# Keys 64-127 meet only tokens 64-127: scores, P times V and k times v as 64x64 quarters, in two parts

## The chip, the core and the metric

The kernel runs on one NeuronCore of a Trainium2 chip. Its engines each work through a queue of their own and meet at semaphores: TensorE (PE, with its weight loads shown apart as PEld), VectorE (DVE), ScalarE (ACT), GpSimd (POOL) and SyncE (SP, which here only issues DMAs). The metric is the device time of one execution in microseconds (us). A profile is one execution in which every instruction's start and end were recorded; its span runs from the first instruction to the last.

## The reference

Two stages, all in float32. The first is an mLSTM cell over 4 batches x 8 heads x 768 tokens, head size 40:

```python
for t in range(S):
    m_new = maximum(f[t] + m, i[t]);  f_s = exp(f[t] + m - m_new);  i_s = exp(i[t] - m_new)
    C = f_s * C + i_s * outer(v[t], k[t]);  n = f_s * n + i_s * k[t]
    y[t] = sigmoid(o[t]) * (C @ q[t]) / maximum(abs(n @ q[t]), 1.0)
```

Its output, as 3072 tokens x 320, goes through a feed-forward layer (FFN): `h = maximum(x @ w_in, 0)`, result `(h * h) @ w_out`, with 2048 hidden columns.

## The kernel before

**Chunks.** The recurrence over tokens is worked in 24 chunks `s` of 128 tokens, 6 to a batch. Within a chunk, key token p acts on token t with the weight exp(A[t] + b[p]) where t is not before p, and with nothing where it is. `A` is a running sum of the gates per head, `b` a per-key term. For each chunk the kernel forms the scores k.q (all keys against all tokens), multiplies them by the weights (this product is called P), multiplies P by v, adds what the state C of earlier chunks gives (q scaled by exp(A), times C), and makes the next C from k times the weighted v. A column of ones beside v carries n along with C. Each chunk's scores are a full 128x128 square per head, half of which the weights set to zero: in the 64x64 quarter of keys 64-127 and tokens 0-63 all of it.

**Chunks 6 to 23**, where the change lies, run in the loop over `parts` (line 1091), four parts to a chunk (`at` = 0 to 3). `s = 6 + n // 4`. Each part also holds a quarter of an FFN stage for an earlier group of two chunks, written as seven products for eight (Strassen's way). In even chunks from 8 on it is the second layer (`ffn2_fast`, products at line 766); in odd ones the first layer (`ffn1_open`, `ffn1_close`, blocks at line 842, and `ffn1_rows`, line 891, which does the last 64 input columns as 64x64 quarters of the array).

**Order.** The program's order on every engine is the order in which it is written; no scheduler moves it. For an even chunk s, part 0 holds `scores(s)` and `weighted(s)`; part 1 begins with `scores(s + 1)` and `attend_turned(s)`; part 2 holds `weighted(s + 1)`. For an odd chunk part 1 begins with the FFN's `ffn1_rows`, then `attend_turned(s)`.

**What the lines do.**
- `load` (line 311), `load_part` (line 943), `load_A` (line 348): DMAs of k, v and of A's rows, the last copied to all 128 partitions (8 heads x 128 tokens each). All are issued on SP. `pair_up` (line 301) copies k and q into a scratch tensor by DMAs of POOL's queue from chunk 10 on; `load_squares` and `turn_kq` make the transposed `kT`, `qT` from it, heads 0-3 in partitions 0-63, heads 4-7 in 64-127.
- `decays` (line 382, ACT): exp(A) in that layout, before the mask; `mask` (line 375, POOL): A is set to -1e30 where the token is before the key; `weigh` (line 390, ACT): exp(A + b), one instruction of 128x128 per head; `values` (line 409, POOL): the weighted v, `vw`.
- `scores` (line 436): from chunk 7 on, 16 matmuls (4 heads of a half x 2 halves of keys x 2 halves of heads), each 40 rows x 64 columns of weights, streaming 128 tokens. Its rows are one partition half and its output another, so four are in the array at a time.
- `weighted` (line 458, DVE): P, two instructions of 128x512.
- `attend_turned` (line 526): 8 matmuls of C (line 543), in quarters; 8 of P times V (line 552), 128 rows of keys x 64 columns, two at a time; 8 of k times v (line 562), 128 rows x 40 columns, streaming 41, two at a time. Then DVE transposes (line 569) and the new C (line 575).
- `store_num`, `load_num`, `normalise_turned`, `store_rows`, `load_rows`, `turn_squares`: the result goes through DRAM to be turned, is normalised and gated, and becomes the FFN's input.
- Before the loop come chunks 0 to 5 with another form of attention, the FFN's first two groups, and the rounding of the weights; `turn_rows(5)` (copy at line 654) and `ffn1_begin` (copies at line 855) stand where the one passes into the other.

PSUM: `ps_at` has three banks (tag "at") for scores and attention's outputs, `ps_h` five in the loop for the FFN and, in part 1, for odd chunks' scores.

Of the kernel before, what the change touches and what calls it, by code (L numbers as in the profile page):

```python
# [17 lines left out]
P = 128  # L18
# [11 lines left out]
def kernel(  # L30
# [64 lines left out]
    A_d = nc.dram_tensor("a_rows", (BH, S), F32, kind="Internal").ap()  # L95

# [157 lines left out]
    eA_T = consts.tile([P, B, NB, H], F32)  # L254

# [42 lines left out]
    KQ_SQ, X_SQ = 7, 6  # L298
    HALVES = slice(0, DP), slice(DP, 2 * DP)

    def pair_up(s):
        b, c = divmod(s, NB)
        eng = nc.sync if s < 10 else nc.gpsimd
        for n, src in enumerate((k, q)):
            for i in range(2):
                eng.dma_start(
                    kq_d[s, i, n].rearrange("j (m r) d -> m j (r d)", r=8),
                    src[b, PR * i : PR * (i + 1), c * P : (c + 1) * P, :].rearrange("j (m r) d -> m j (r d)", r=8),
                )

    def load(s):
        b, c = divmod(s, NB)
        (dk, sk), nat_q, vv = load_parts(s)
        for dst, src in ((dk, sk), nat_q, vv) if s < KQ_SQ else ((dk, sk), vv):
            nc.sync.dma_start(dst, src[b, :, c * P : (c + 1) * P, :].rearrange("h p d -> p h d"))
# [32 lines left out]
    def load_A(s):  # L348
# [3 lines left out]
        d["A"] = [A]  # L352
        nc.sync.dma_start(
# [21 lines left out]
    def mask(s):  # L375

        A = st[s]["A"][0]
        nc.gpsimd.affine_select(  # L378
            A[:], A[:], compare_op=ALU.is_ge, fill=-1e30, base=0, pattern=[[0, H], [1, P]], channel_multiplier=-1,
        )  # L380

    def decays(s):

        if s % NB > 0:
            e = st[s]["eA"] = kq_b[2 + s % 2][:, 1].rearrange("p (j two) d -> p j (two d)", two=2)
            for i in range(2):
                rows = slice(DP * i, DP * (i + 1))
                nc.scalar.activation(e[rows], st[s]["A"][0][rows, PR * i : PR * (i + 1), :], AF.Exp)  # L388

    def weigh(s, masked=False):  # L390
# [8 lines left out]
        for i in range(len(A)):  # L399
# [9 lines left out]
    def values(s):  # L409
        b, c = divmod(s, NB)  # L410
        d = st[s]
        if c + 1 < NB:
            d["vw"] = prep.tile([P, H, D1], F32, name="vw")
            nc.gpsimd.tensor_tensor(  # L414
# [21 lines left out]
    def scores(s, o=(False, False)):  # L436
# [4 lines left out]
        if s >= KQ_SQ:  # L441
            for j in range(PR):
                for keys in HALVES:
                    for i in range(2):
                        rows = slice(DP * i, DP * i + D)
                        nc.tensor.matmul(  # L446
                            sc[i][keys, j, :], lhsT=d["kT"][rows, j, keys], rhs=d["qT"][rows, j, :], start=(j == 0),
                            stop=True, skip_group_check=True,
                        )
# [8 lines left out]
    def weighted(s):  # L458
        d = st[s]
        d["P"] = []  # L460
        for i in range(2):
            heads = slice(i, H, 2) if s < KQ_SQ else slice(PR * i, PR * (i + 1))
            t = d["W"][:, heads, :]
# [4 lines left out]
            nc.vector.tensor_tensor(t, d["sc"][i], d["W"][:, heads, :], op=ALU.mult)  # L468
# [57 lines left out]
    def attend_turned(s):  # L526

# [3 lines left out]
        halves = [slice(DP * i, DP * (i + 1)) for i in range(2)]  # L534
        live = [slice(DP * i, DP * i + D) for i in range(2)]
        numT = [ps_at.tile([P, W], F32, name="numT", tag="at")[:].rearrange("p (c t) -> p c t", t=P) for _ in range(2)]

        if c > 0:
            C = C_b[(s - 1) % 2]
            for e in range(2):  # L540
                for i, g in ((0, 0), (1, 1), (0, 1), (1, 0)):
                    j = 2 * e + g
                    nc.tensor.matmul(  # L543
                        numT[i][halves[g], e, :], lhsT=C[live[i], j * D1 : j * D1 + DP], rhs=d["eA"][live[i], j, :],
                        start=(e == 0), stop=False, skip_group_check=True,
                    )
        for i in range(2):
            for e in range(2):
                for g in range(2):
                    j = 2 * e + g  # L550
                    h = PR * i + j
                    nc.tensor.matmul(  # L552
                        numT[i][halves[g], e, :], lhsT=va_w[s % NKQ][:, h * D1 : h * D1 + DP],
# [675 lines left out]
```

## Time and profile before

| what | value |
|---|---|
| median of 6 runs | 503.38 us (501.31 to 504.5) |
| the profiled execution | 502.71 us, span 500.9 us |
| PE busy | 493.3 us (98%) |
| DVE / ACT / POOL busy | 354.4 (71%) / 249.2 (50%) / 151.1 us (30%) |
| DMA | 67.75 MB, mean 135 GB/s; 185600 of 235551 packets under 512 B |

A matmul of the code is two records of PE and two of PEld, since float32 is passed twice. Matmuls overlap in the array: a record's own length (0.27 us for a quarter) is longer than the step from one group to the next, so the starts are read, not the lengths. The "idle before" of a group counts only while its engine had nothing; an idle engine off the path costs nothing. Line numbers are those of the kernel before unless a text says otherwise.

### The profile page before, as it was taken

To read this page: it belongs to the slowest core of one execution; us is meant where nothing else is said; L and a number is where in the kernel's file an instruction comes from. 1 tells how busy PE (TensorE), PEld (TensorE's weight loads), DVE (VectorE), ACT (ScalarE), POOL (GpSimd) and SP (SyncE) were. 2 spreads that over 40 slices of the span, in tenths; PEclk is the share of its full clock that TensorE was granted. 3 is DMA by queue.
4 is the path that set the end of the run, shared out by engine and by line. 5 is a ranking of instruction groups with operands and counts; after the bars stand their busy time and mean duration, and the time that the engine had idled before them with its cause. 6 is when DMAs were issued, how large, how long until landed. Compare 5 with 4: busy or idle time off the path is not lost.

```text
span 500.9 us, 13846 instructions
## 1 busy us (share of the span) xinstructions
PE 493.3 (98%) x5640; PEld 458.0 (91%) x5641; DVE 354.4 (71%) x646; ACT 249.2 (50%) x492; POOL 151.1 (30%) x194
## 2 busy tenths in 40 slices
PE   9989999999999999999999999999999999999997
PEld 4877878897799999999999999999999999999997
DVE  8589969879967866767867856867857956735441
ACT  3867878854541660771661770561871560423400
POOL 3355733431525224215225224234224031020000
PEclk9998999999999999999999999999999999999999
DMA  9999898855778758767758757767745522200000
GB/s 190 216 227 214 241 217 156 223 97 98 158 158 167 152 118 173 158 140 161 157 114 178 156 112 170 165 127 170 160 96 141 114 67 65 61 23 14 1 27 27
DMA packets 235551, 67.75 MB, mean 135 GB/s; under 512 B 185600, under 2 KB 229120, under 8 KB 235488
## 3 DMA queue, kind: packets, MB, share of 16 engines
q1 hardware_dynamic: 233600, 62.09, 59.2%
q0 software_dynamic: 1792, 4.59, 3.1%
q8 instruction: 44, 0.72, 0.6%
q10 hardware_dynamic: 96, 0.20, 0.1%
q14 instruction: 19, 0.16, 0.1%
HBM read 54.56 MB, written 17.86 MB: 145 GB/s over the span
## 4 chain that ended last, share of the span: by engine, by line
PE 91%; DVE 5%; DMA 2%; ACT 1%; issue 1%; SPq 0%; DVEq 0%
PE h_ps L766 34%; PE h_ps L842 25%; PE h_ps L891 8%; PE numT L552 4%; PE h_ps L712 4%; PE h_ps L675 3%; PE hp L491 2%; PE h_ps L446 2%; PE tp L446 2%; PE numT L543 1%; PE tp L454 1%; DVE mag L225 1%; DMA va<-in_v_dram 1%; PE dC L562 1%; PE A_ps L369 1%; PE tp L431 1%
## 5 line engine op out<-in xcount | busy, mean ns | idle before, releaser
L378 POOL TENSOR_SCALAR_AFFINE_SELECT A_bc<-A_bc 128x1024 f32<-128x1024 f32 x22 | 27.1, 1234 | 108.5 <-ACT kq L388 87.0
L766 PE MATMUL h_ps<-T,S 128*128 128x160 f32 x352 | 51.4, 299 | 0.0
L872 ACT COPY r_sb<-h_ps 128x512 f32<-128x512 f32 x18 | 10.5, 586 | 81.8 <-PE h_ps L842 81.8
L766 PE MATMUL h_ps<-w_out,g 128*128 128x160 f32 x336 | 49.2, 303 | 0.0
L782 DVE TENSOR_TENSOR y_sb<-y_sb,h_ps 128x160 f32<-128x160 f32 x44 | 14.1, 320 | 49.6 <-PE h_ps L766 49.6
L766 PEld LDWEIGHTS h_ps<-T,S 128*128 128x128 f32 x352 | 49.0, 190 | 0.0
L766 PEld LDWEIGHTS h_ps<-w_out,g 128*128 128x128 f32 x336 | 46.1, 190 | 1.4 <-issue 1.2
L402 ACT ACTIVATE A_bc<-A_bc,b_T 128x128 f32<-128x128 f32 x144 | 44.0, 388 | 5.3 <-POOL A_bc L378 5.0
L842 PE MATMUL h_ps<-xT,w_in 128*128 128x128 f32 x320 | 42.8, 278 | 0.0
L842 PE MATMUL h_ps<-lent_t,w_in 128*128 128x128 f32 x320 | 42.2, 275 | 0.0
L842 PEld LDWEIGHTS h_ps<-xT,w_in 128*128 128x128 f32 x320 | 38.9, 192 | 1.1 <-issue 0.7
L891 PE MATMUL h_ps<-xT,w_in 64*64 64x128 f32 x960 | 39.4, 273 | 0.0
L842 PE MATMUL h_ps<-lent_t 128*128 128x128 f32 x320 | 39.0, 275 | 0.0
L842 PEld LDWEIGHTS h_ps<-lent_t,w_in 128*128 128x128 f32 x320 | 38.9, 192 | 0.0
L842 PEld LDWEIGHTS h_ps<-lent_t 128*128 128x128 f32 x320 | 37.3, 192 | 0.0
L891 PEld LDWEIGHTS h_ps<-xT,w_in 64*64 64x64 f32 x960 | 34.6, 133 | 2.4
L569 DVE STREAM_TRANSPOSE tn<-numT 128x256 f32<-128x256 f32 x36 | 16.0, 450 | 28.8 <-PE numT L552 28.8
L414 POOL TENSOR_TENSOR vw<-va,A_bc 128x328 f32<-128x328 f32 x15 | 13.7, 913 | 72.5 <-issue 38.1
L909 DVE TENSOR_TENSOR r_sb<-r_sb,h_ps 128x512 f32<-128x512 f32 x20 | 13.8, 688 | 23.7 <-PE h_ps L842 14.3
L675 PE MATMUL h_ps<-xT,w_in 128*128 128x256 f32 x128 | 29.8, 386 | 0.6 <-ACT xT L654 0.6
L766 PE MATMUL h_ps<-w_out,g_c 128*128 128x160 f32 x192 | 28.0, 302 | 0.0
L675 PEld LDWEIGHTS h_ps<-xT,w_in 128*128 128x128 f32 x128 | 24.1, 193 | 4.1 <-ACT xT L654 0.8
(190 smaller groups left out, 1115.5 us busy)
## 6 DMA issues: line engine op xcount, KB each, us to landing
A_bc<-a_rows SPq DMA_DIRECT2D x22, 512.0 KB, 5.0
num_rows<-tn SPq DMA_DIRECT2D x18, 256.0 KB, 2.2
kq<-num_rows SPq DMA_DIRECT2D x72, 64.0 KB, 1.9
raw<-in_moe_w_out_dram SPq DMA_DIRECT2D x7, 640.0 KB, 4.2
kqT<-kq_rows SPq DMA_DIRECT2D x34, 128.0 KB, 3.0
kq<-in_k_dram SPq DMA_DIRECT2D x24, 160.0 KB, 3.8
va<-in_v_dram SPq DMA_DIRECT2D x24, 160.0 KB, 5.1
og<-in_o_gate_dram SPq DMA_DIRECT2D x24, 160.0 KB, 4.8
```

What stands on the lines that cost most here:

```text
L378: nc.gpsimd.affine_select(A[:], A[:], compare_op=ALU.is_ge, fill=-1e30, base=0, pattern=[[0, H], [1, P]], channel_multiplier=-1,)
L402: nc.scalar.activation(d["W"][:, i * n + h, :], A[i][:, h, :], AF.Exp, bias=b_T[:, b, c, i * n + h : i * n + h + 1],)
L446: nc.tensor.matmul(sc[i][keys, j, :], lhsT=d["kT"][rows, j, keys], rhs=d["qT"][rows, j, :], start=(j == 0), stop=True, skip_group_check=True,)
L552: nc.tensor.matmul(numT[i][halves[g], e, :], lhsT=va_w[s % NKQ][:, h * D1 : h * D1 + DP], rhs=d["P"][h % 2][:, h // 2, :] if s < KQ_SQ els ...
L569: nc.vector.transpose(to[:, 2 * i : 2 * i + 2], numT[i][:, :2, :].rearrange("p c t -> p (c t)"))
L675: nc.tensor.matmul(hs[i][:, n, :], lhsT=w_in[:, a, fb * P : (fb + 1) * P], rhs=xT[:, :, a, :], start=(n == 0 and a == 0), stop=False,)
L712: nc.tensor.matmul(o_ps, lhsT=st["g2", g][:, fb, j * P : (j + 1) * P], rhs=w_out[:, fb, :], start=(fb == 0), stop=(fb == NF - 1),)
L766: nc.tensor.matmul(to, lhsT=lhsT[:, p], rhs=rhs[:, p, :], start=(start and p == 0), stop=(p == NPAIR - 1), skip_group_check=True,)
L782: add = lambda to, a, b: nc.vector.tensor_tensor(to, a, b, op=ALU.add)
L842: nc.tensor.matmul(to[:, n, :], lhsT=lhsT[:, 4 * q + n, :], rhs=rhs, start=(start and n == 0), stop=True, skip_group_check=True,)
L891: nc.tensor.matmul(to[cols, n, :], lhsT=w_in2[rows, 4 * q + n, cols], rhs=rhs, start=(start and n == 0), stop=True, skip_group_check=True,)
L909: tt(U2[:], U2[:], Y[:], op=ALU.add)
```

## The change

From chunk 8 on (`ROT = 8`), keys 64-127 are multiplied with tokens 64-127 only, and scores, P times V and k times v are all cut into 64x64 quarters of the array. To fill four quarters at once, the data are laid out anew:

- Heads are numbered anew within their halves (`pair_up` takes every second head).
- `load_k` swaps the two token halves of heads 4-7 (three DMAs for one); `load_v` puts v into slots by key half (four DMAs for one, on SP for chunks 8 to 10, on POOL's queue from 11 on; issued a part later than before in half of the chunks).
- A's rows stand in a second scratch tensor `a_slots`, which three DMAs of POOL's queue fill per batch (`spread_slots`), before the loop, and in chunks 8 and 12; `load_A` reads it in two DMAs of contiguous rows.
- `mask` is two instructions of 64 partitions; `weigh` is 4 instructions of 128 columns and 4 of 64, with biases from a table `b_R`, which four ACT copies of 64x96 make just before the loop; `decays` is four instructions of half the width; `weighted` works on 384 columns instead of 512; `normalise_turned` has two more DVE instructions.

On PE `attend_turned` becomes two parts. `attend_begin`: half of C's matmuls, P times V of the early keys' pairing (wide), half of k times v. `attend_end`: the other half of k times v, the late keys' P times V (64 columns), the other half of C. Both parts add into the same PSUM bytes from different row halves of the array. Between them stands other PE work: the scores of the odd chunk in even chunks, `ffn1_rows` in odd ones, nothing in chunk 7. A DVE instruction on one element, issued at the end of `attend_begin`, reads from the first part's output; the first instruction of the second part that overwrites that place waits for it. Chunks 6 and 7 take the two parts too, at full width.

The core of the diff:

```diff
@@ scores
         if s >= KQ_SQ:
-            for j in range(PR):
-                for keys in HALVES:
-                    for i in range(2):
-                        rows = slice(DP * i, DP * i + D)
-                        nc.tensor.matmul(sc[i][keys, j, :], lhsT=d["kT"][rows, j, keys], rhs=d["qT"][rows, j, :], ...)
+            for e in range(2):
+                for late_keys in range(2):
+                    for c in range(2):
+                        for i in range(2):
+                            rows = slice(DP * i, DP * i + D)
...
+                                j, keys = 2 * (c ^ late_keys) + e, HALVES[late_keys]
+                                to = d["sc"][i][HALVES[c], e, slice(0, DP) if late_keys else slice(DP, 3 * DP)]
+                                t0 = DP * late_keys
+                            nc.tensor.matmul(to, lhsT=d["kT"][rows, j, keys], rhs=d["qT"][rows, j, t0:], ...)
@@ attend_turned becomes attend_begin and attend_end
+    def attend_begin(s):
...
+        out = d["out"] = [ps_at.tile([P, W], F32, name="numT", tag="at") for _ in range(2)]
...
+        if c > 0:
+            values_of_C(s, (0, 1))
+        for i in range(2):
+            values_of_P(s, i, (0, 1), False)
+        if c + 1 < NB:
+            new_C(s, (0, 1), False)
+            end, spare = out[1][DP : DP + 1, 2 * P + D1 : 2 * P + D1 + 1], d["kq"][DP : DP + 1, 0, 2, DP - 1 :]
+        else:
+            end, spare = out[1][DP : DP + 1, P : P + 1], C_b[(s - 1) % 2][0:1, 4 * D1 : 4 * D1 + 1]
+        nc.vector.tensor_scalar(spare, end, scalar1=0.0, scalar2=None, op0=ALU.mult)
...
+    def values_of_P(s, i, rows, second):
+        d = st[s]
+        t0 = DP if second and s >= ROT else 0
+        for e in range(2):
+            for m in range(2):
+                at, keys = slot(s, m, e, i, second), HALVES[rows[m]]
...
+                nc.tensor.matmul(
+                    d["numT"][m][HALVES[e], i, t0:], lhsT=va_w[s % NKQ][keys, at * D1 : at * D1 + DP], rhs=rhs, ...)
+
+    def new_C(s, rows, second):
+        d = st[s]
+        for e in (1, 0) if second else (0, 1):
+            for i in range(2):
+                for m in range(2):
+                    keys = HALVES[rows[m]]
+                    nc.tensor.matmul(
+                        d["dC"][m][HALVES[i], e, :], lhsT=d["kq"][keys, 0, 4 * m + 2 * e + i, :],
+                        rhs=d["vw"][keys, slot(s, m, e, i, second), :], start=False, stop=True, ...)
+
+    def attend_end(s):
...
+        if c + 1 < NB:
+            new_C(s, (1, 0), True)
+        else:
+            values_of_C(s, (1, 0), (1, 0))
+        for i in (1, 0):
+            values_of_P(s, i, (1, 0), True)
+        if 0 < c < NB - 1:
+            values_of_C(s, (1, 0))
@@ load_k, load_v, spread_slots, load_A
+        nc.sync.dma_start(dst[:, :PR], src[:, :PR])
+        for n in range(2):
+            nc.sync.dma_start(dst[HALVES[n], PR:], src[HALVES[1 - n], PR:])
...
+        eng = nc.sync if s < 11 else nc.gpsimd
+        for n in range(2):
+            for late_keys in range(2):
+                m = n ^ late_keys
+                eng.dma_start(dst[HALVES[n], PR * (1 - late_keys) : PR * (2 - late_keys)],
+                              src[HALVES[late_keys], PR * m : PR * (m + 1)])
...
+        nc.gpsimd.dma_start(A_slots[b].rearrange("c m x own t -> (m x) c own t")[:, :, 1], rows)
+        for m in range(2):
+            nc.gpsimd.dma_start(to[1 - m][:, :, 0], rows[PR * m : PR * (m + 1)])
...
+            for m in range(2):
+                nc.sync.dma_start(A[HALVES[m]].rearrange("p h t -> p (h t)"),
+                    A_slots[b, c, m].rearrange("x own t -> (x own t)").unsqueeze(0).to_broadcast([DP, H * P]))
@@ weigh, weighted
+        for x in range(PR if s >= ROT else 0):
+            for own, to in enumerate((slice(DP, P), slice(P, 2 * P))):
+                nc.scalar.activation(A[0][:, x, to], A[0][:, x, to], AF.Exp, bias=b_R[:, b, c, own, x : x + 1])
...
-            nc.vector.tensor_tensor(t, d["sc"][i], d["W"][:, heads, :], op=ALU.mult)
+            nc.vector.tensor_tensor(t, d["sc"][i], d["W"][:, heads, :] if s < ROT else t, op=ALU.mult)
@@ before the loop
+    for m in range(2):
+        for own in range(2):
+            x = PR * (m ^ own ^ 1)
+            nc.scalar.copy(b_R[HALVES[m], :, :, own], b_T[HALVES[1 - own], :, :, x : x + PR])
+    spread_slots(1)
@@ the loop, part 1
         if at == 1:
+            do(attend_begin, s)
             if even:
                 do(lambda s: scores(s, ("h", "h")), s + 1)
             if fast:
                 ffn1_rows(g, 0, True)
-            do(attend_turned, s)
+            do(attend_end, s)
...
-                do(lambda s: load_part(s, 0), s + 4)
+                do(load_k, s + 4)
...
         if s > 6 and at == (3 if even else 2):
             do(pair_up, s + 3)
+            do(load_v, s + 4)
+        if n in (9, 25):
+            spread_slots(2 + n // 25)
```

## The prediction

> **What bounds the kernel now.** I read first the page: busy shares, slices, the chain that ended last.
>
> ```profile
> span 500.9 us, 13846 instructions
> PE 493.3 (98%) x5640; PEld 458.0 (91%) x5641; DVE 354.4 (71%) x646; ACT 249.2 (50%) x492; POOL 151.1 (30%) x194
> ...
> PEclk9998999999999999999999999999999999999999
> ...
> PE 91%; DVE 5%; DMA 2%; ACT 1%; issue 1%; SPq 0%; DVEq 0%
> ```
>
> TensorE is busy 98% of the span, holds 91% of the chain, and its granted clock stays at full speed. "Busy" is modelled, so I asked next for PE's waits: over the span five, 4.4 us together, all in lines of the opening part (484, 653, 675, the idle matmuls); from 100 us to the end, not one. From there the time is the sum of PE's steps: what PE saves comes off the end, unless a new wait appears. So I took the steps from PE's timeline around chunk 14 (its first column is the start; the next line's start minus a line's own is the step that counts).
>
> ```profile
> 253.81 1.10 PE L446 MATMUL h_ps<-kqT 40*64 40x128 f32 x32
> 254.74 0.62 PE L543 MATMUL numT<-kq,C 40*64 40x128 f32 x16
> 255.28 1.09 PE L552 MATMUL numT<-A_bc,va 128*64 128x128 f32 x16
> 256.21 0.48 PE L562 MATMUL dC<-vw,kq 128*40 128x41 f32 x16
> 256.62 4.61 PE L766 MATMUL h_ps<-w_out,g 128*128 128x160 f32 x32
> ```
>
> The reader is to see: 16 matmuls of the code are 32 records (two passes, each with its weight load); scores take 0.93 us, C 0.54, P times V 0.93, k times v 0.41. In the same timeline the FFN rows (line 891, quarters of 64x64) start four at a time at 247.52, 247.63, 247.74 ... 248.18: a group of four quarters, 128 columns wide, takes 0.109. Scores are 8 such groups (0.87) and 0.05 of entry; C 4 groups (0.44) and 0.10 of leaving the quarter form; P times V 8 pairs at 0.109 and 0.05 of entry; k times v 8 pairs at 0.039 and 0.10 of leaving.
>
> How fast can a narrow group go? Two views: line 491 early in the run (41 columns streamed, 128 columns of weights), and the weight loads at the head of the scores, asked for up to 253.86 and up to 253.90.
>
> ```profile
> 21.24 1.92 PE L491 MATMUL hp<-va,g_c 128*128 128x41 f32 x16
> 22.98 1.10 PE L477 MATMUL hi<-C_sb,kqT 128*128 128x82 f32 x8
> ```
> ```profile
> 253.81 0.15 PEld L446 LDWEIGHTS h_ps<-kqT 40*64 40x64 f32 x4 [0.17 <-issue]
> ```
> ```profile
> 253.81 0.21 PEld L446 LDWEIGHTS h_ps<-kqT 40*64 40x64 f32 x8 [0.17 <-issue]
> ```
>
> Line 491 takes 1.74/16 = 0.109 a step although only 41 columns stream: there the weight load sets the pace. Line 562, with 40 columns of weights, steps at 0.039. And a second group of four 64-column loads ends 0.06 after the first.
>
> **The change, part by part.** The widths: a narrow quarter group (64 or 41 columns streamed, 64 of weights) is not in the trace. Between 0.039 (40 weight columns) and 0.109 (128) a line gives 0.058 at 64; half of 0.109 is 0.055; the loads gave 0.06. I take 0.057, nearest to all three. Ends: 0.053, and 0.109, the only pace that groups of four do show.
>
> *Scores, chunks 8-23.* 8 wide groups become 4 wide and 4 narrow: 0.872 to 0.664, -0.21 a chunk.
> *P times V.* 8 pairs of full height become 4 wide and 4 narrow groups: -0.21 a chunk.
> *k times v.* 8 pairs at 0.039 (0.31) become 8 narrow groups (0.46), since all 64 columns of k are loaded now: +0.15, in every chunk but 11, 17 and 23, which have no new C.
> *Form of the array.* All of attention is now 64x64, like the FFN rows and the scores beside it: the switch between C and P goes (0.10 + 0.05), the leave at the end stays: -0.15 a chunk.
> Chunk with new C: -0.42, 13 of them; without: -0.57, three. Sum -7.1. Chunks 6 and 7 get the new form without narrow P or scores: -0.15 + 0.15, nothing.
>
> *The hand-over.* A one-element read on DVE ends the first part; the second part's first k times v waits for it. Its price is the length of the last matmul (0.20, line 562), DVE's start after PE, the read, and PE's start after DVE.
>
> ```profile
> 261.27 0.32 DVE L782 TENSOR_TENSOR y_sb<-y_sb,h_ps 128x160 f32<-128x160 f32 x1 [2.46 <-PE h_ps L766]
> ...
> 267.52 0.20 DVE L600 RECIPROCAL dm<-dm 128x8 f32<-128x8 f32 x1
> ```
>
> Line 766 ends at 256.62 + 4.61 = 261.23 and DVE starts at 261.27: 0.04. The read: as other small operations, 0.20 (line 600). PE's start after DVE: no row; 0 to 0.2, I take 0.06, near the other direction. Together 0.5. Even chunks cover it with the odd scores (0.66), odd ones with the FFN rows (1.75). DVE must be free: in even chunks it idles 1.67 us before line 569; in odd ones its sum of line 761 ends at 272.29, when the first part ends too. Without cover this costs 0.45 a chunk. Chunk 7 has nothing between the parts: +0.45, and 0.05 for its late weighting: +0.5 (0.3 to 0.8). Behind the read on DVE stand the two transposes and the C sums; they start when PE ends the chunk, about 256.2, as now; PE needs neither before the next chunk.
>
> *b_R.* Four copies of 64x96 are put into ACT's order between these:
>
> ```profile
> 98.16 0.46 ACT L654 COPY xT<-tp 128x384 f32<-128x384 f32 x1
> 98.74 0.59 ACT L855 COPY r_sb<-h_ps 128x512 f32<-128x512 f32 x1
> 99.63 0.59 ACT L855 COPY r_sb<-h_ps 128x512 f32<-128x512 f32 x1 [0.31 <-PE h_ps L842]
> ```
>
> PE's 17th matmul of line 842 adds to the tile that the first line 855 copies; at 0.112 a record from 97.55 its turn comes at 99.4, just after the copy's end at 99.33: no slack. Each copy costs 0.2 to 0.29 (128x160 takes 0.29 on lines 786 and 791), so PE waits 0.8 to 1.1: I take 0.8; floor 0.
>
> *POOL.* Chunks 11 on get v by four DMAs on POOL's queue, plus three times three for a_slots.
>
> ```profile
> 266.23 1.05 POOL L306 DMA_DIRECT2D kq_rows<-in_k_dram  x2
> ...
> 271.18 2.05 POOL L378 TENSOR_SCALAR_AFFINE_SELECT A_bc<-A_bc 128x1024 f32<-128x1024 f32 x1 [2.89 <-ACT kq L388]
> ```
> ```profile
> 279.41 2.45 ACT L402 ACTIVATE A_bc<-A_bc,b_T 128x128 f32<-128x128 f32 x8
> ```
>
> An issue of line 306 takes 0.52 for 64 runs; v has 256 runs: 0.52 to 2.1 each, 2 to 8.3 us a chunk. Behind them stands the mask; from 268.3 to the weighing at 279.41 are 11.1 us, less 2.05 for the mask: 9.0 of cover. Cost nothing; beyond 2.25 an issue it would run into the weighing. The mask in two halves of a quarter of the elements each: same total, 1.1 to 2.1.
> *SP* issues three k loads for one and two A loads for one (0.4 to 0.7 each); after k it waits for num_rows to land, until 259.09 from 257.74, and that hides two. Four v issues on SP for chunks 8-10 stand before the loop's end; nothing PE needs within a chunk is behind them.
> *ACT* weighs 25% fewer elements (2.45 to about 2.0) and spreads the decays over four instructions (1.28 to at most 2.5); the mask starts up to 1.2 later, the weighing at most 0.5. *DVE*: weighting -25% of 1.28, normalising two more small operations (0.2 each), the read 0.2: about even at 71% busy. A's rows come as 4 KB runs, not 512 B: less DMA work, and PE waits for none.
>
> **Sum.** -7.1 + 0.5 + 0.8 = -5.8 us, against the profiled execution's 502.71 (span 500.9 and 1.8 outside): 496.9. The median shown, 503.38, is 0.7 above it: 497.6.
>
> A rule that speaks against this: the Trainium skill (TensorEngine Tiling (Array Packing), Instruction Overhead) gives every matmul some 60 cycles, so that a free dimension of 1 takes as long as 60, and warns against tiling a dimension that is already small. At the 2.4 GHz of TensorE: Matmul & The Clock Gate (its table of specs) that is 25 ns, an estimate of 0.100 for four in a row; 248 narrow groups would then make the sum +4.9, 508.3. Line 562 does two matmuls in 0.039, under 20 ns each, so I hold to the row.
>
> **Rivals.**
> *Narrow groups don't run at under 0.08* (slower side; at 0.109 the change does not do what it says). There are 128 in scores and P, 104 + 16 in k times v: 248, each 0.01 of pace worth 2.5 us. From 0.080 the gain is gone; at 0.109 the time is 510.5. For it: eight instructions a group would follow at 7 ns, and the fastest stretch of over 100 in the trace is the FFN rows, 128 in 1.75 us, 14 ns each. Against: those are held by width, and line 562 issues 32 in 0.31.
> *The hand-over is not covered in even chunks.* Only 0.16 is to spare; if the round trip takes 0.75, 8 chunks lose 0.25 each: 499.7. For it: PE's start after DVE is unmeasured. Against: DVE is idle there.
> *POOL falls behind:* at 3 us an issue the weighing is 3 us late, and with it ACT's squares behind it, which the next FFN part waits for: at most 3 us in each of 8 pairs of chunks, 522. Against: 2.1 is already the row scaled by the number of runs.
>
> **How the numbers follow.** Forecast 0.74 (own range 496.0 to 499.5: pace 0.053 to 0.063, copies 0 to 1.1, spread of the runs 1.6). Hand-over 0.12. Narrow groups over 0.074: 0.10, of which 0.03 end within 0.3% of before; POOL 0.02; a rest of 0.02 halved between same and slower. A difference under 0.3% (1.5 us) can't be told from none. The range 495.5 to 501.2 leaves out the two slower rivals and the fastest tail. Faster 0.74 + 0.12, same 0.03 + 0.01, slower 0.07 + 0.02 + 0.01.
>
> **What would show it.** Scores at 0.98 now falling to about 0.77 where they stand alone; P in two lines of about 0.44 and 0.23; k times v in two of 0.23; no wait of PE on DVE in even chunks, one of 0.5 in chunk 7; a PE wait on ACT of 0.8 near 99.4 (line 855's copies); no further PE wait. Narrow groups stepping at 0.08 or more, or PE waits on DVE or POOL in each chunk, would prove it wrong.

## The result, and the profile after

The changed kernel takes 507.62 us (median of 30 runs, 501.33 to 512.51), the kernel before 503.79 us (65 runs, 501.28 to 506.85); the ratio is 1.0049, with a 95% interval of 1.0033 to 1.0064. It is slower by half a per cent by this ratio, by 0.8% by the medians; the ratio leaves out the seven slowest of the 30 runs, over 1.5% above the fastest, whose mean granted clock was 0.982 to 0.987, that of the four quickest 0.990 to 0.993. I had forecast 497.6 us, in a range of 495.5 to 501.2. The profiled execution is one of the quicker ones, 504.57 us, against 502.71 us before. Two traces also differ by a few us ahead of the change, in part by stretches of half TensorE clock there (between 0 and 10.2 us of them in the profiles below). I therefore compare the traces over one stretch: from the first score matmul of chunk 6 to the end of the last matmul. That is 401.35 us before and 403.62 us after, 2.27 us more. By the medians the loss is 3.8 us; what makes a median execution lose more than the profiled one, no profile here shows.

The page of the changed kernel:

```profile
span 502.8 us, 15197 instructions
PE 491.1 (98%) x6168; PEld 456.9 (91%) x6169; DVE 346.1 (69%) x700; ACT 249.4 (50%) x524; POOL 192.5 (38%) x271
...
PEclk9998999999799999999999999999999999999999
...
PE 77%; DVE 7%; DMA 5%; ACT 4%; SPq 3%; issue 2%; POOL 0%; DVEq 0%; POOLq 0%; ACTq 0%
```

PE is as busy as before, but the chain that ended last now runs 77% through PE instead of 91%: DVE, DMA, ACT and SP have a larger part in it. And there is a new 7 in the clock, about 125 us in. The waits of PE, over the span:

```profile
PE numT L632 <- DVE A_bc L548: 2.7, 1, 2.7
...
PE h_ps L962 <- ACT r_sb L975: 0.8, 1, 0.8
PE numT L662 <- DVE kq L624: 0.7, 3, 0.3
```

Three kinds of wait are new. The second was forecast, the third in part, the first, which is the largest, not at all. The steps themselves did what was forecast. The timeline of PE in chunk 14 (first column the start):

```profile
257.94 0.45 PE L632 MATMUL numT<-kq,C 40*64 40x128 f32 x8
258.21 0.62 PE L651 MATMUL numT<-A_bc,va 64*64 64x128 f32 x16
258.65 0.39 PE L662 MATMUL numT<-vw,kq 64*64 64x41 f32 x16
258.85 0.88 PE L526 MATMUL h_ps<-kqT 40*64 40x128 f32 x32
259.55 0.40 PE L662 MATMUL numT<-vw,kq 64*64 64x41 f32 x16
259.76 0.44 PE L651 MATMUL numT<-A_bc,va 64*64 64x64 f32 x16
260.02 0.40 PE L632 MATMUL numT<-kq,C 40*64 40x128 f32 x8
260.35 0.95 PE L886 MATMUL h_ps<-w_out,g 128*128 128x160 f32 x5
```

From start to start: odd scores 0.70 (0.93 before), P times V 0.44 and 0.26, k times v 0.20 and 0.21, C 0.27 and 0.33. Together 2.41 us from the first C to the FFN; before, the same work took 2.81. Two chunks, with the scores of both, save 0.80 us where nothing waits, and 0.95 where one of them has no new C.

So the gain is there, 6.8 us over chunks 8 to 23 (the last kernel below, in which nothing waits there, has it in full), and some 9 us are lost around it. Where they are lost, in us (each column is the time between two score starts, or to the end, from PE's timeline):

| kernel | chunk 6 to chunk 8 | chunk 8 to chunk 16 | chunk 16 to end | sum |
|---|---|---|---|---|
| before | 39.82 | 149.57 | 211.95 | 401.35 |
| after | 47.14 | 146.41 | 210.07 | 403.62 |

Up to chunk 8, where of the narrow quarters only those of k times v in chunks 6 and 7 have run, the changed kernel is 7.3 us behind. PE's timeline at the start of chunk 7:

```profile
121.59 0.43 PE L632 MATMUL numT<-kq,C 40*64 40x128 f32 x2
124.67 0.49 PE L632 MATMUL numT<-kq,C 40*64 40x128 f32 x3 [2.65 <-DVE A_bc L548]
```

PE waits for weighted(7). Upstream on DVE:

```profile
114.44 0.69 DVE L596 TENSOR_TENSOR kq<-kq,kqT 128x512 f32<-128x512 f32 x1
117.90 0.17 DVE L714 TENSOR_SCALAR dm<-kq 128x8 f32<-128x8 f32 x1 [2.77 <-DMA kq<-num_rows]
...
123.93 1.28 DVE L548 TENSOR_TENSOR A_bc<-tp,A_bc 128x512 f32<-128x512 f32 x2
```

normalise_turned(6) (line 714) waits 2.77 us for load_num(6) to land, and everything behind it on DVE, weighted(7) last, is as late. Before, the same two stood at 114.60 and 120.50:

```profile
114.60 0.17 DVE L598 TENSOR_SCALAR dm<-kq 128x8 f32<-128x8 f32 x1
...
120.50 1.28 DVE L468 TENSOR_TENSOR A_bc<-tp,A_bc 128x512 f32<-128x512 f32 x2
```

And upstream of that, SP's queue, first after, then before:

```profile
108.69 0.34 SPq L697 DMA_DIRECT2D num_rows<-tn  x1
109.13 0.39 SPq L327 DMA_DIRECT2D kq<-in_k_dram  x1
109.61 1.31 SPq L329 DMA_DIRECT2D kq<-in_k_dram  x2
111.02 3.20 SPq L339 DMA_DIRECT2D va<-in_v_dram  x4
114.27 2.02 SPq L702 DMA_DIRECT2D kq<-num_rows  x4
```
```profile
107.60 0.35 SPq L581 DMA_DIRECT2D num_rows<-tn  x1
108.05 0.39 SPq L315 DMA_DIRECT2D kq<-in_k_dram  x1
108.54 0.63 SPq L315 DMA_DIRECT2D va<-in_v_dram  x1
109.83 1.75 SPq L586 DMA_DIRECT2D kq<-num_rows  x4
```

load(10) stands between store_num(6) and load_num(6). It was two DMAs and 1.1 us of issue, which fitted into the landing of store_num; it is seven now, 5.1 us, and load_num starts 5.6 us after store_num instead of 2.2. That is the reading I then tested, together with two more that the same trace offers: the half clock behind the wait, and the one-element read, which in chunks 10, 16, 18 and 20 comes late because it is queued behind DVE's sums.

### The profile page after: what moved, and what is told of

The parts are those of the page before. It is cut to its first block, busy times and chain, and to the rows that moved or that the text cites. A ratio compares the mean times of both kernels' runs of the same rounds, so it can differ in the third digit from the quotient of the medians.

```text
span 502.8 us, 15197 instructions
## 1 busy us (share of the span) xinstructions
PE 491.1 (98%) x6168; PEld 456.9 (91%) x6169; DVE 346.1 (69%) x700; ACT 249.4 (50%) x524; POOL 192.5 (38%) x271
## 4 chain that ended last, share of the span: by engine, by line
PE 77%; DVE 7%; DMA 5%; ACT 4%; SPq 3%; issue 2%; POOL 0%; DVEq 0%; POOLq 0%; ACTq 0%
PE h_ps L886 31%; PE h_ps L962 20%; PE h_ps L1011 6%; PE h_ps L795 3%; PE h_ps L832 3%; DMA kqT<-kq_rows 3%; PE numT L651 2%; PE numT L632 2%; PE numT L662 1%; PE hp L571 1%; SPq L702 1%; DVE mag L226 1%; DMA num_rows<-tn 1%; PE tp L534 1%; DMA kq<-in_q_dram 1%
## 5 line engine op out<-in xcount | busy, mean ns | idle before, releaser
L427 POOL TENSOR_SCALAR_AFFINE_SELECT A_bc<-A_bc 64x512 f32<-64x512 f32 x32 | 25.2, 787 | 73.5 <-ACT kq L444 72.1
L457 ACT ACTIVATE A_bc<-A_bc,b_R 128x64 f32<-128x64 f32 (+1 forms) x128 | 35.7, 361 | 1.8 <-POOL A_bc L427 1.4
L682 DVE STREAM_TRANSPOSE tn<-numT 128x256 f32<-128x256 f32 x36 | 14.0, 428 | 28.3 <-PE numT L632 19.5
L339 POOL DMA_DIRECT2D va<-in_v_dram x52 | 31.9, 621 | 1.3 <-issue 1.3
L477 POOL TENSOR_TENSOR vw<-va,A_bc 128x328 f32<-128x328 f32 x13 | 10.1, 775 | 55.3 <-ACT A_bc L457 55.2
```

Source lines behind the costliest of these rows:

```text
L339: eng.dma_start(dst[HALVES[n], PR * (1 - late_keys) : PR * (2 - late_keys)], src[HALVES[late_keys], PR * m : PR * (m + 1)],)
L427: nc.gpsimd.affine_select(part, part, compare_op=ALU.is_ge, fill=-1e30, base=0, pattern=[[0, PR], [0, 2], [1, DP]], channel_multiplier=-1,)
L457: nc.scalar.activation(A[0][:, x, to], A[0][:, x, to], AF.Exp, bias=b_R[:, b, c, own, x : x + 1],)
L477: nc.gpsimd.tensor_tensor(d["vw"][:].rearrange("p (own x) d -> p own x d", own=2), d["va"][:].rearrange("p (own x) d -> p own x d", own=2) ...
L682: nc.vector.transpose(to[:, 2 * m : 2 * m + 2], d["numT"][m].rearrange("p c t -> p (c t)"))
```

## The experiments

Theory A: SP's longer queue in chunk 6, the wait, and a half clock brought on by it. Rival B: the clock falls for some other reason. Rival C: the quarters and the hand-over themselves cost it. Two more theories came up on the way: D, the hand-over read ties PE to what DVE has queued ahead of it, and E, SP's chain of issues and landings is what makes DVE late.

### The swap in chunk 6

```diff
-                do(load, s + 4)
                 do(load_num, s)
+                do(load, s + 4)
                 do(pair_up, s + 3)
```

> The changed kernel with one swap on SP in chunk 6: load_num(6), the four read-backs of the numerator, goes ahead of load(10), which is now seven DMAs. Theory A (the queue): load_num(6) was held up by the seven issues, normalise_turned(6) came 3.3 us late on DVE, weighted(7) behind it kept PE waiting 2.9 us in chunk 7, and that idle time set the granted clock to a half for two stretches of 3.41 us, another 3.4 us lost. With the swap both go: 504.57 less 2.9 less 3.4 is about 498.3 (497 to 499.5), the wait of L632 for A_bc is gone from the waits of PE, and the clock is 1 after 60 us. Rival B (the clock drops for another reason, by chance or because PE is busier): the wait goes, the half clock stays somewhere: 501 to 504. Rival C (the cost is in the quarters and the hand-over themselves): 505 to 508, no change.

505.14 us, 1.0057 of before [1.0026, 1.0087]. Chunk 7's wait for L632 and the half clock behind it are gone, as A has it (6 to 8 takes 41.68 us instead of 47.14), and yet only 2.5 us of the time went. A's time, 497 to 499.5, is missed, and the time itself lies where C put it. Other waits took the place of the one in chunk 7. The waits of PE:

```profile
PE numT L662 <- DVE kq L624: 2.3, 4, 1.6
PE numT L651 <- DVE A_bc L548: 1.3, 1, 1.3
...
PE numT L632 <- DVE A_bc L548: 0.8, 1, 0.8
```

PE arrives 5 us earlier in chunk 8 and meets a DVE that is late there too: chunks 8 to 16 take 150.54 us, 4.1 us more than in the changed kernel. The late start in chunk 8 had hidden that. The swap has a price of its own, too: SP now stands still for 1.7 us in chunk 6 until store_num(6) has landed, and issues k and v of chunk 10 only then. The timeline of DVE ahead of the 1.6 us:

```profile
143.79 1.47 DVE L867 TENSOR_TENSOR w_out<-w_out 128x1280 f32<-128x1280 f32 x1
145.18 1.21 DVE L881 TENSOR_TENSOR g<-g 128x1024 f32<-128x1024 f32 x1
146.31 0.32 DVE L902 TENSOR_TENSOR y_sb<-h_ps,y_sb 128x160 f32<-128x160 f32 x1
146.66 0.16 DVE L624 TENSOR_SCALAR kq<-numT 1x1 f32<-1x1 f32 x1
```

The hand-over read (line 624) stands behind three other instructions. PE's next matmul waits for it, and so for all of them.

### The seven DMAs alone, in the kernel before

```diff
+        if s == 10:
+            for (dst, src), cuts in (((dk, sk), (0, 3, 6, 8)), (vv, (0, 2, 4, 6, 8))):
+                for h0, h1 in zip(cuts, cuts[1:]):
+                    nc.sync.dma_start(dst[:, h0:h1], src[b, h0:h1, c * P : (c + 1) * P, :].rearrange("h p d -> p h d"))
+            return
```

> The kernel before, with nothing but load(10) cut into seven DMAs by heads (three of k, four of v) where it stood as two. Theory A: the same hold-up as in the changed kernel: load_num(6) some 4 us later, PE waits 2 to 3 us at the start of chunk 7's C products, and the clock falls to a half behind it: 503.8 plus 2.9 plus 3.4 is about 510; with the wait alone, without the clock, 506.5. Rivals B and C: 503.8, no change, since no quarter and no hand-over is in it.

506.69 us, 1.0081 [1.0053, 1.0108], slower without a single quarter of this change. The seven are cut by heads here and take SP 3.6 us, not 5.1. PE waits 1.7 us for the weighted products of chunk 7 ("numT L548 <- DVE A_bc L473" in its waits), and 6 to 8 takes 41.86 us, 2.04 more than before; behind it nothing changes by more than 0.01, and what the profiled run is longer besides lies ahead of chunk 6, which the edit does not touch. C falls as the cause of chunk 7. The half clock did not come in this profile: 1.7 us of idle time did not bring it on, so the figure with the wait alone, 506.5, is the nearer one. That it fits so well is in part luck: it had 2.9 us for the wait, the trace has 2.0, and the medians differ by 3.6.

### Fillers instead of idle time

```diff
+        for _ in range(7 if s == 7 else 0):
+            nc.tensor.matmul(
+                out[0][:], lhsT=zeros[:, :1].to_broadcast([P, P]), rhs=zeros[:, :1].to_broadcast([P, W]), start=True, stop=True,
+            )
```

> The changed kernel with seven filler products of zeros (128x512 in bf16, 0.38 us each in the first 30 us of the trace, 2.7 us) on PE ahead of chunk 7's C products: the wait for weighted(7) stays, but PE is busy through most of it. Theory A in both its terms: the clock stays at 1, and 3.4 us of the changed kernel's time go: 507.6 to about 504.2 by medians, 501.2 by the profiled execution. If the clock falls for another reason (rival B) or if the half clock costs nothing because PE is waiting anyway: 507 to 508, no change, and the half stretches are still there behind 124 us.

By medians inconclusive: 506.77 us, 1.0068 [1.0039, 1.0096], less than 1 us below the changed kernel, where A had 3.4. The profile shows the mechanism: with PE busy for part of the wait (1.4 us of it are left idle) there is no half clock behind it. Weighted(7) comes as late as in the changed kernel (PE resumes 8.8 us after the scores of chunk 7, 8.6 there), and chunk 6 to chunk 8 still takes 44.79 us instead of 47.14. So the half clock cost about 2.6 us (2.35 and the 0.25 that weighted came later), not the 3.4 I had put on it. What was saved is given back in part behind it: chunk 8 to chunk 16 takes 147.96 us instead of 146.41, with a new wait of 0.8 us for weighted in chunk 10.

### The b_R copies out of the way

The swap, and:

```diff
-    for m in range(2):
-        for own in range(2):
-            x = PR * (m ^ own ^ 1)
-            nc.scalar.copy(b_R[HALVES[m], :, :, own], b_T[HALVES[1 - own], :, :, x : x + PR])
...
+        if n == 3:
+            ...
```

> The swap of chunk 6 on SP, and the four b_R copies on ACT moved from ahead of the loop to the end of chunk 6's first quarter of the following FFN part (n = 3), where nothing on PE waits behind them. Theory A: the step of 1.0 us at 99.8 us (PE waiting for a relu behind the copies) goes as well: 1.0 below the kernel with the swap alone, about 497.3. Rival: something else that ACT or DVE owes PE is due at the same place and takes the wait's place: 0 to 0.3 below it.

503.98 us, 1.0005 [0.9978, 1.0033]: 1.2 us below the swap alone, as A has it, though the two intervals overlap. The step of 1.1 us near 99.8 us is gone, chunk 6 to chunk 7 takes 19.22 us (20.26 in the changed kernel, 19.20 before). This profile loses it again from chunk 8 to chunk 16 (152.35 us, with waits of 1.0 and 1.6 us and a stretch of half clock), so that the traces show the copies' step and not a gain over the whole.

### DVE's sums behind the hand-over read

```diff
             do(attend_begin, s)
+            if n == 9:
+                sums_of_weights(3)
+            if which == 2 and g > 0:
+                sums(g, slice(0, NPAIR), (3,))
...
-        if n == 8:
-            sums_of_weights(3)
-            sums(1, slice(0, NPAIR), (3,))
...
-        if which == 2 and g > 1 and i < 2:
-            sums(g, slice(0, NPAIR), (3 + i,))
+        if which == 2 and g > 1 and i == 1:
+            sums(g, slice(0, NPAIR), (4,))
```

> The changed kernel with DVE's order in the even chunks changed alone: the sum A21 = A11 - A21 of the FFN's fast products (L881, 1.20 us; in chunk 8 the sum of weights L867, 1.47 us, as well) is put behind the hand-over read of attend_begin instead of ahead of it. Theory D (the hand-over ties PE to DVE's queue): the read came late because it stood behind L881 and L902, and the steps into the second k x v in chunks 10, 16, 18 and 20 (0.13, 0.38, 0.38, 0.25 us, and 0.05 each for the switch) fall to 0.04: about 1.3 us less behind chunk 9, with chunk 7's wait and the half clock left as they are: 507.6 to about 506.3 by medians. Rival: DVE is late as a whole, and the read is waited for as before or the weighted products behind it are: no change, and the waits of L662 for kq stay at 0.7.

509.69 us, of two runs only, so the time says little. The waits say what matters:

```profile
PE numT L632 <- DVE A_bc L548: 4.1, 2, 2.7
PE numT L651 <- DVE A_bc L548: 1.5, 1, 1.5
...
PE numT L662 <- DVE kq L624: 0.3, 1, 0.3
```

The hand-over's waits in the even chunks are gone, so D had their place right. But PE then waits for the weighted products in chunks 12 and 20 (1.5 and 1.4 us). With the swap and the copies as well:

> All three together: load_num(6) ahead of load(10), the b_R copies out of PE's way, and the sums behind the hand-over read. Theory D with A: the profile of the kernel with the swap alone had its waits moved to the hand-over of chunk 8 (1.6 us behind L867, L881 and L902) and to weighted(12) (1.3 us, DVE waiting for a landing); the first goes, the second may stay: 503.98 less 1.6 less 0.5 is about 502 by medians, 499 where the clock stays at 1. Rival E (DVE's lateness comes from SP and the DMAs, and the read is only where it shows): the wait moves on to the transposes or to weighted, and it stays at 503.5 to 504.5.

503.54 us, 0.9986 [0.9952, 1.0020], nothing measurable against 503.98 without the sums, as rival E has it. A wait taken off the hand-over comes up at weighted, a few us on, because DVE itself is late. Why is it?

### load_num ahead of load_k in every chunk

```diff
             if s > 6:
-                do(load_k, s + 4)
                 do(load_num, s)
+                do(load_k, s + 4)
                 do(load_squares, s + 2)
```

> The same, with load_num ahead of load_k in the chunks from 7 on as well: three k issues (1.9 us on SP in the trace) leave the chain store_num, load_num, normalise_turned. Theory E (SP's order of issues is what makes DVE late): normalise comes 1 to 2 us earlier in each chunk and the waits for weighted go: 1 to 2 us below the run with the three, 500 to 501. Theory D alone: the same as the run with the three, within 0.5. Third case: load_squares and load_A, which are no earlier or later by it, hold the transposes of k and q: the same or 0.5 above.

521.31 us, 1.0349 [1.0302, 1.0397]: wrong in sign. PE waits for weighted in chunks 8 to 20, five times for 1.9 us or more, and each of these five waits has a stretch of half clock behind it. SP's waits between 136 and 364 us show why:

```profile
SPq L758 <- DMA x_rows<-x_sb: 23.5, 7, 5.6
SPq L702 <- DMA num_rows<-tn: 21.6, 11, 3.6
```

load_num must wait for store_num to land, about 2 us; with the k loads put behind it, SP stands still for that time and issues them afterwards. SP's queue is a chain with two such landings in each chunk, store_rows to load_rows and store_num to load_num, and what stands between them is their cover. The swap in chunk 6 had the same flaw. This was the turn: not fewer issues in one place, but issues under both landings. The same view of the changed kernel and of the kernel before:

```profile
SPq L758 <- DMA x_rows<-x_sb: 27.5, 12, 4.0
...
SPq L702 <- DMA num_rows<-tn: 0.8, 4, 0.2
```
```profile
SPq L586 <- DMA num_rows<-tn: 18.4, 12, 2.8
...
SPq L638 <- DMA x_rows<-x_sb: 5.8, 7, 1.1
```

Before, SP waited 18.4 us for num_rows and 5.8 for x_rows. In the changed kernel the k loads cover num_rows almost to the full (0.8 us), but v's issue, moved to POOL, no longer covers x_rows: 27.5 us. One landing got too much cover, the other lost it, and it also takes longer than before (median from issue to landing 3.9 us, 2.5 before).

### v on POOL, and all the transfers, in the kernel before

The first has four v loads on POOL behind pair_up, cut by heads, where one stood on SP, from chunk 11 on; v of chunks 8 to 10 stays as it was, one DMA each on SP:

```diff
-        do(lambda s: load_part(s, 2), s + 4)
...
+            do(load_v, s + 4)
```

> The kernel before with nothing changed but its v loads from chunk 11 on: four DMAs on POOL behind pair_up, where the changed kernel has them, instead of one on SP (chunks 8 to 10 on SP, in four). It has no hand-over, so that DVE's queue does not reach PE within a chunk. Theory E: store_rows lands later (2.5 us before, 3.9 in the changed kernel, with v's pieces beside it), SP's chain behind it is later, and if PE has no slack for that it waits: 504 to 507. Theory D: DVE and SP get later, nothing on PE waits: 503.1, within 0.5.

503.88 us, 1.0027 [1.0009, 1.0046], and no wait on PE behind 70 us: from chunk 6 to the end 401.36 us, 401.35 before. SP waits 18.6 us for x_rows instead of 5.8, and PE does not see it, as D has it. store_rows lands in 2.6 us here, so that v's pieces on POOL are not what makes it 3.9 in the changed kernel; nor are all the transfers of the next run (2.8), and the cause of that later landing stays open. In the profiled execution all that it is longer lies ahead of chunk 6, where the clock is at half for 10.2 us instead of 3.4. The second adds the seven DMAs of chunk 6 and three k loads for one from chunk 7 on; the loads of chunks 8 and 9 and A's rows stay as before:

```diff
-                do(lambda s: load_part(s, 0), s + 4)
+                do(load_k, s + 4)      # heads 0-3, 4-5, 6-7
```

> The kernel before with the changed kernel's transfers alone: load(10) in seven DMAs in chunk 6, three k loads between store_num and load_num from chunk 7 on, v in four DMAs on POOL from chunk 11 on (cut by heads, the same bytes in the same places). No quarters, no hand-over, no new tiles. Theory E: the transfers alone make it slower: 3.6 us as with the seven DMAs of chunk 6 alone, the 0.8 of v on POOL, and 0 to 3 more where DVE waits for load_num's landing: 507 to 510, DVE waiting for num_rows in several chunks. Theory D (it takes the hand-over to bring DVE's lateness to PE): 506.5 to 507, PE waiting in chunk 7 only.

505.97 us, 1.0041 [1.0015, 1.0066]; chunk 6 to the end 403.34 us, 1.99 more than before, all of it up to chunk 8, around chunk 7's wait of 1.7 us. D has this one by the place, with a time 0.5 us below its range: DVE waits for num_rows in two chunks only (2.4 us in all) and nothing behind chunk 8 reaches PE. At the pace of the kernel before SP still keeps up.

### SP spread over both landings

```diff
     def load_k(s):
         ...
         nc.sync.dma_start(dst[:, :PR], src[:, :PR])
+
+    def load_k_turned(s):
+        ...
         for n in range(2):
             nc.sync.dma_start(dst[HALVES[n], PR:], src[HALVES[1 - n], PR:])
...
                 do(load_o, s + 5)
+            do(load_k_turned, s + 4)
             do(load_rows, s)
             if s == 6:
                 do(load_A, s + 2)
+                do(load_v, s + 4)
```

> The changed kernel with its SP queue spread alone: the two turned k loads (L329, 0.68 us each) leave the place between store_num and load_num for the place between store_rows and load_rows, where v's issue stood before and where SP now waits 2.3 us a chunk for store_rows to land; in chunk 6 v(10) goes behind load_rows(6) and load_A(8) as well. Theory E (SP's chain store_rows, load_rows, store_num, load_num, load_squares is what the change lengthened, by 2 k issues of 0.68 and a landing of 1 to 2 us that lost its cover): load_num is 1.4 us earlier in each chunk and about 4 us earlier in chunk 6, DVE's waits for num_rows and kq_rows between 136 and 364 us (10 us in the changed kernel) shrink to 2 or less, chunk 7's wait goes with its half clock, and it takes 499 to 502. What stays are the b_R copies (1.0) and the hand-over behind DVE's sums (1.3 to 3). Theory D alone (DVE's order, not SP's): chunk 7's wait goes, 504 to 505 as with the swap.

501.71 us, 0.9963 [0.9933, 0.9994]: 5.9 us below the changed kernel with the same transfers, and below the kernel before. Chunk 7's wait for weighted and its half clock are gone, and chunk 6 to the end takes 399.81 us. The time is within theory E's range, but DVE's waits for num_rows only shrank to 7.5 us from 60 to 440 us (10.4 in the changed kernel), not to 2 or less; the 2.8 us ahead of normalise_turned(6) went. With the copies and the sums as well:

> The same with the b_R copies out of PE's way and the sums behind the hand-over read. If SP (E) and the hand-over (D) are both causes and nothing third stands behind them, the whole gain of the quarters comes out: 503.1 less 7.1 plus 0.5 for chunk 7's hand-over is 496.5, within 495.5 to 498.5, and PE has no wait over 0.5 us behind 60 us. If it stays at 499 or above, a third holder is left, and the waits of PE name it. Theory E alone (the hand-over is no cause once SP is on time): the same as the spread alone less 1.0.

501.81 us, 0.9959 [0.9930, 0.9989], not 496.5. In the profile the stretch is 397.38 us, 2.4 us shorter than with the spread alone; the medians do not show it. What is left on PE behind 70 us is 0.3 and 1.1 us for weighted in chunks 7 and 10 and 0.3 us for the hand-over in chunk 7, and DVE still waits for landings there: a holder was left. My reading was SP again, held by x_rows (10.2 us between 136 and 364 us) ahead of store_num.

### load_rows under store_num's landing

```diff
             do(store_num, s)
+            if s > 8:
+                do(load_rows, s - 1)
             if s > 6:
                 do(load_k, s + 4)
                 do(load_num, s)
...
-            do(load_rows, s)
+            if s < 8:
+                do(load_rows, s)
```

and turn_squares(s - 1) one part later in the odd chunks.

> The run with SP spread, b_R copies moved and sums moved, and from chunk 8 on load_rows(s) deferred from the end of chunk s to chunk s+1, between store_num(s+1) and load_num(s+1), where its four issues (2.7 us) cover store_num's landing; turn_squares moves one part later in the odd chunks. Theory E to its end: what is left over the steps' sum is SP, which waits 10 us for x_rows and 18 us for num_rows to land between 136 and 364 us; with the first wait gone store_num goes out when tn is ready, 1.5 to 2 us earlier, DVE's waits for num_rows (7.4 us) shrink, and the wait of 1.1 us for weighted in chunk 10 goes: 1 to 2 us less from the scores of chunk 6 to the last product, 500 to 501 by medians. Rival: load_rows is then late for turn_squares, DVE waits for x_rows instead and hands that to PE by the hand-over read and the weighted products: 502 to 505.

499.05 us, 0.9888 [0.9857, 0.9919], 1.1% faster than before (five runs) and the best kernel here, 1 us better than I had expected. DVE's waits for num_rows between 136 and 364 us fall from 7.0 to 3.7 us. The rival's wait does come, 3.0 us of DVE for x_rows to come back, but it does not reach PE. Among PE's waits one lies behind 70 us, the hand-over of chunk 7 (the lines are those of this kernel):

```profile
PE numT L669 <- DVE kq L631: 0.3, 1, 0.3
```

SP has turned from late to early; its waits between 136 and 364 us are now for DVE's own results:

```profile
SPq L704 <- DVE C L696: 29.4, 8, 5.8
SPq L704 <- DVE C L700: 10.5, 2, 5.7
```

| kernel | chunk 6 to chunk 8 | chunk 8 to chunk 16 | chunk 16 to end | sum |
|---|---|---|---|---|
| before | 39.82 | 149.57 | 211.95 | 401.35 |
| after | 47.14 | 146.41 | 210.07 | 403.62 |
| swap in chunk 6 | 41.68 | 150.54 | 210.47 | 402.69 |
| SP spread | 41.76 | 148.86 | 209.19 | 399.81 |
| and copies, sums | 41.17 | 147.77 | 208.45 | 397.38 |
| and load_rows deferred | 40.80 | 146.24 | 208.45 | 395.49 |

The last line of the table is 5.86 us below before, with the quarters as the change made them: 6.83 us gained from chunk 8 on, 0.98 lost in chunk 7. There the hand-over takes a step of 0.51 us, and two steps of 0.2 us come from the two halves of weighted(7), still a little late.

## Why the prediction was wrong

**The step that failed** is the one on SP: "Four v issues on SP for chunks 8-10 stand before the loop's end; nothing PE needs within a chunk is behind them", costed at nothing. load(10), which chunk 6 issues, puts three of k and four of v there. load_num(6) is behind them, and normalise_turned(6), DVE's queue and weighted(7) behind that. The words "within a chunk" were the slip: PE needed it one chunk later, and DVE had no room (between lines 714 and 548 of the changed kernel it has no idle time). Seven DMAs at that place in the kernel before cost PE 2.0 us; the changed kernel's cost it 2.9 us (3.08 us from line 632's start to its resumption, of which some 0.15 is work). That k's extra issues are covered "until 259.09 from 257.74" was true of num_rows and left out what v's issue had covered.

**The clock was not in the sum.** I had treated a wait as its own length. 2.65 us of idle time took another 2.6 us with it by two stretches of half clock; the 2.6 comes from one profile, that of the fillers.

**The pace of narrow groups** held: forecast 0.057, measured 0.057 for scores (two groups in 0.114 in chunk 14), 0.058 for the second k times v and P together (eight groups in 0.467), 0.051 for the first k times v with its 41 columns. The rival that groups would run at 0.08 or more falls, and so does the estimate of 0.100 from the Trainium skill's TensorEngine Tiling (Array Packing), Instruction Overhead: four quarters of 64 columns start within 0.057 us, and the measurement decides. That 508.3, the time worked out from that estimate, is near the measured 507.62 is chance: the pace that it rests on is not in the trace. The sum of the steps was 7.1 us; the last kernel of the table gains 6.83 from chunk 8 on.

**The hand-over** was priced right where DVE is idle, 0.5 us and covered in chunks 8, 12, 14 and 22 and in the odd ones; in chunk 7 its step is 0.57 us at half clock and 0.51 at full. The 0.05 for chunk 7's late weighting was too little: some 0.4 even in the last kernel. In chunks 10, 16, 18 and 20 it waits behind line 881's sum and line 902, 0.13, 0.38, 0.38 and 0.25 us and 0.05 each for leaving and entering, 1.3 us in all. "DVE is idle there" was read from one chunk. The timeline of DVE in chunk 16:

```profile
295.27 1.21 DVE L881 TENSOR_TENSOR g_c<-g_c 128x1024 f32<-128x1024 f32 x1
296.39 0.31 DVE L902 TENSOR_TENSOR y_sb<-h_ps,y_sb 128x160 f32<-128x160 f32 x1
296.74 0.16 DVE L624 TENSOR_SCALAR kq<-numT 1x1 f32<-1x1 f32 x1
```

The rival on the hand-over had the place right and the reason wrong (a slow round trip); it came to 1.3 us beside the 2.0 I gave it. Its sum was not sound either: a price of 0.75 against a cover of 0.66 loses 0.09 a chunk, not 0.25.

**b_R.** Forecast 0.8 us near 99.4; measured a wait of 0.8 and a step of 1.10 instead of 0.11 at 99.8, so that the four copies of 0.27 us cost 1.0.

**POOL.** An issue of v takes 0.62 us, within 0.52 to 2.1, and nothing waits for it. What I had missed is the other side of that move, v's issue no longer under x_rows' landing on SP.

The sum as it was: -6.8 for the steps, +1.0 copies, +2.9 wait, +2.6 half clock, +0.6 hand-over in chunk 7, +1.3 in four even chunks, +0.5 in chunks 16 and 18, where weighted is late (in 16 the first C and P take 0.95 instead of 0.71, in 18 the first P 0.71 instead of 0.49), together +2.1; measured +2.27, so that some 0.2 us is not traced. With the waits taken out one by one the stretch comes to -5.86. For a kernel without the copies the forecast's terms give -7.1 + 0.5 = -6.6; 0.3 of the difference is the steps and 0.5 chunk 7. The steps were right, their cover was not. The second part without any hand-over was not tried, because the two parts would then race; the read's own price over a whole run stays an inference from the steps.

## What to carry to other kernels

When PE sets the time, a change that adds DMAs has to be followed down the issuing queue to the next instruction in it that anything waits for, over the next chunk too, and with what the moved issue had been covering. Making PE quicker shortens every other engine's time to keep up (with most of the changed kernel's transfers at the old pace, nothing behind chunk 8 reached PE): a wait that is removed or hidden by lateness comes up somewhere else until the queue with the landings in it is given slack. And a read that ties PE to another engine in mid-stage costs what that engine has queued ahead of it, which is to be looked up in every chunk and not in one.

## What the runs showed of the hardware

A long wait of PE cost more here than its idle time. Over all these profiles, behind 116 us, every idle stretch of 1.9 us or more (seven: 1.91 to 2.68 us) was followed by one or two stretches of 3.41 us at half the granted clock, which began between 0.5 us before the wait's end and 1.2 us after it. Of the shorter ones from 0.8 us on (sixteen, up to 1.70 us) one of 1.60 us was followed by two, and a pair of 0.96 and 1.58 us within 5 us by one; the others, a second one of 1.60 and those of 1.66 and 1.70 us among them, by none. The windows of the changed kernel's trace around chunk 7 (start and end, length, busy us of PE, PEld, DVE, ACT and POOL, then TensorE clock, DMA share and GB/s):

```profile
120.70:124.10 3.40, 1.32 (x6) 0.56 (x4) 3.37 (x7) 0.05 (x1) 1.54 (x1) 1.00 0.94 148
124.20:127.60 3.40, 2.66 (x62) 2.51 (x66) 1.17 (x3) 3.32 (x4) 0.00 (x0) 0.50 0.66 91
127.60:131.00 3.40, 3.40 (x28) 2.37 (x23) 2.08 (x5) 1.13 (x4) 0.58 (x1) 0.50 0.64 175
131.00:134.40 3.40, 3.40 (x14) 2.40 (x13) 3.37 (x4) 0.31 (x2) 2.31 (x3) 1.00 0.57 129
```

The clock is down for 6.8 us, nearly all of it while PE is at work again. Why 1.60 us was enough once and not the other time, nor 1.70 us, is open: it was not tried whether it matters where the idle time falls against the grid of 3.41 us.
